# A transformer block on one core: gate and query rows by column groups, first statistics from products of tokens, and another order

## The chip, the core and the metric

The kernel runs on one core of a Trainium2 chip. The metric is device time in microseconds (us), here of that single core. PE is TensorE (matrix products), ACT is ScalarE, DVE is VectorE, POOL is GpSimd, and SP is the queue that issues nearly all DMA transfers. PSUM is the memory that PE writes; this kernel divides its eight banks into four pairs, numbered 0 to 3.

## The reference, cut to what matters

```python
# x: 2048 tokens of 576; 32 heads of 18; the feed-forward is 4608 wide; c is one row of 576
mod = silu(c) @ w_mod                       # six rows: sa, ca, ga, sb, cb, gb
h = layernorm(x) * (1 + ca) + sa
q, k, v = split_heads(h @ wqkv)
phi_q = [softmax(q @ w_phi), softmax(-(q @ w_phi))]      # 36 features a head
phi_k = the same of k
kv, z = phi_k^T v, sum of phi_k over the tokens
x = x + ga * (((phi_q @ kv) / (phi_q . z + 1e-6)) @ wo)
h = layernorm(x) * (1 + cb) + sb
out = x + gb * (relu(h @ w1) @ w2)
```

## The kernel before

The 2048 tokens are 16 tiles of 128. The kernel has two stages.

**The ordered stage** is everything up to the attention of the first two tiles. It is a string ORDER of some 450 short job names, executed from left to right. Each job emits its instructions on its own engine, so ORDER fixes the order on every engine, and semaphores do the rest. `name:n` gives a job PSUM pair n; a job that takes a pair waits until the pair's former contents have been read. The numbers are token tiles or weight chunks:

- `Z` idle products of 512 columns that keep PE going; `sc`, `sh` the columns ca and sa of mod; `FK` folds w_phi into the key weights, `fs fsr` evict them scaled by 1 + ca, `frd fra frr` unscaled (d on DVE, a on ACT); `FQ`, `FQs`, `FQrd`, `FQra` the same for the query weights, by chunk; `wsd` scales the value weights.
- `bn` layernorm statistics of a tile from x_sb on DVE (L238, L239), `sa sp` their roots on ACT and POOL, `T Tc` turn them into four rows that are appended to the fifth chunk of the transposed tokens. The matching rows of the weights come from `KR VR QR` (products), `KRh VRh QRh` (ACT copies), `KRd VRd QRd` (DVE, L467, straight into the weights).
- Per tile: `K` keys (10 products of 288 columns, L271; tiles 0 and 1 as `Ka` and `Kb`), `eK` two exponentials on ACT (L276), `sK` sums of 18 on DVE (L281), `rK` reciprocals on ACT, `pA pM` on POOL, `V` values, `vE` their eviction on DVE (L302), `kv` their product (L321). `kz` ends that sum.
- `Q` queries of a tile, `eQ` their exponentials, `sq` (L333) the write of these to DRAM and `qi` (L336) the read back, each 288 KB on SP's queue. `qs qp qt` finish a tile on DVE, POOL and SP. Six slots of EQ hold the exponentials of Q; slots 4 and 5 are the same bytes as the places that `qi` of tiles 3 and 4 fills.
- `ga gb` the gate rows (10 products each, L357), `gac gbc` their copies (L361) and `wo` wo scaled by ga on POOL (L602); `m2` mod for the second layernorm; `nu nO ot oc W lb lr ap xc ht hd ha` take tiles 0 and 1 through attention, output product and second layernorm to h2, which the feed-forward reads; `wl w2a w2b` load w1 and w2; `tp` differences of w2 on DVE.

**The feed-forward stage** runs over eight blocks b of two tiles: `l1` (L641, L648) and `l2` (L700). Hooks in `l1` of block b finish the queries of the next two tiles (`q_fin`: sum on DVE, product on POOL, transpose by DMA), read later ones back, and compute their attention. At its head stands, before the change, the read back of tiles 3 and 4:

```python
    NB = NT // 2
    for u in range(QF + 1, QF + NL):
        q_in(u)
    for b in range(NB):
```

In l1, the group's DVE step (L657) must have read a PSUM pair before PE's next group enters it.

Of the kernel before, what the change touches and what calls it, by code (L numbers as in the profile page):

```python
# [7 lines left out]
P = 128  # L8
BF16 = mybir.dt.bfloat16
FP32 = mybir.dt.float32  # L10
FP16 = mybir.dt.float16
EPS = 1e-5
ACT = mybir.ActivationFunctionType
ALU = mybir.AluOpType
AXX = mybir.AxisListType.X

S, D, H, DH, DFF = 2048, 576, 32, 18, 4608
NT = S // P
NC = 5
R = 116  # L20
F = NC * R
X0 = 96
NX = X0 + 4
NJ = DFF // P
HD = 288
G6 = ((0, 6), (6, 6), (12, 4), (16, 6), (22, 6), (28, 4))
GR = 108
# [13 lines left out]


ORDER = """
Z11 sx sd rp sc Z2 ca FK Z3 frd2 fs3 fs0 frd1 sh fs2 fsr fs4 frd0 fs1 frr fra4 Ka0:0 shc bn1 fra3 VR:2 wsd4
bn0 KR:1 bn2 sa0 Z6 sp0 KRh wsd2 bn3 KRd sa2 bn4 VRh T0:1 sp2 Z2 Tc0 VRd Kb0 T2:1 Z1 eKa0 wsd3 Ka1:2 wsd0 wsd1
bn5 Kb1 Tc2 V0:0 eKa1 sK0 K3:1 sa4 sK1 rK0 sp4 K2:2 eK3 pA0 pM0 vE0 bn7 T4:0 rK1 V1:1 Tc4 pA1 eK2 sK3 pM1 K4:0
vE1 rK3 kv0 eK4 K5:2 pA3 bn9 pM3 sK2 kv1 eK5 FQ4:1 FQ3:0 FQrd4 FQra3 ga:2 sK4 FQs4 rK2 V2:1 gac bn6 pA2 pM2
FQs3 V4:2 bn8 sa6 rK4 sp6 vE2 V3:0 sa8 pA4 pM4 vE4 T6:1 kv2 vE3 Tc6 FQ0:2 K6:1 wl0 FQs0 FQrd0 sp8 wo3 sK5 kv3
eK6 kv4 wo2 K7:0 bn10 rK5 wo1 T8:2 wl1 gb:1 sK6 Tc8 eK7 pA5 pM5 K8:2 bn13 rK6 gbc K9:0 sK7 wo4 eK8 V5:1 pA6
bn11 pM6 eK9 V6:2 sK8 wo0 rK7 V7:0 vE5 rK8 pA7 sa10 vE6 pA8 pM8 kv5 FQ1:1 vE7 V8:2 FQs1 sK9 FQra1 sp10 V9:0  # L50
pM7 vE8 rK9 T10:1 kv6 bn12 Tc10 FQ2:2 pA9 K10:1 wl2 pM9 FQs2 FQrd2 sa12 vE9 kv7 eK10 K11:2 sp12 bn15 T12:0 kv8
sK10 Tc12 kv9 eK11 K12:1 bn14 V10:0 rK10 eK12 sK11 pA10 pM10 V11:2 vE10 rK11 QR:1 sa14 pA11 sK12 pM11 kv10 wl3
QRh V12:0 vE11 rK12 sp14 QRd pA12 kv11 pM12 vE12 T14:2 Q0:1 Tc14 wl4 K14:2 eQ0 kv12 Q1:0 eK14 qs0 Q2:1 eQ1
sK14 qp0 K15:2 eQ2 qs1 K13:0 eK15 sq2 m2:1 qp1 qi2 eK13 sK15 V13:2 qt0 qt1 w2a0 rK14 sK13 m2c pA14 V14:0 pM14 rK15 rK13
V15:1 vE14 pA13 pM13 vE13 Q3:0 Q4:2 eQ3 pA15 pM15 vE15 kv13 kv14 eQ4 Q5:1 sq3 kv15 eQ5 Q6:0 kz sq4
Q7:2 eQ6 w2a1 sq5 nu1:3 Q8:1 eQ7 nO1 nu0:0 tp0 eQ8 ot1:3 Q9:2 nO0 sq6 w2a2 oc1 sq8 Q10:1 eQ9 sq7 ot0:0 W1:3
w2b2 oc0 tp1 eQ10 W0:2 lb1 sq9 xc1 Q11:0 lr1 lb0 w2b0 xc0 ap1 tp2 Q12:1 lr0 w2b1 eQ11 ap0 ht1:3 sq10 hd1 ha1 ht0:2 sq11
Q13:0 ha0 hd0 Q14:3 eQ13 Q15:2 eQ12 sq13 eQ15 sq12 eQ14 sq15 sq14
"""

@with_exitstack
def tile_block(ctx, tc, a, out):
# [4 lines left out]
    dram = ctx.enter_context(tc.tile_pool(name="dram", bufs=1, space=bass.MemoryType.DRAM))  # L67
    psum = ctx.enter_context(tc.tile_pool(name="ps", bufs=1, space=bass.MemoryType.PSUM))

    def small(shape, dtype, name):  # L70
        return mem.tile(shape, dtype, name=name, tag=name)

    def carve(reg, start, shape):
        n = 1
        for d in shape:
            n *= d
        names = "abcd"[:len(shape)]
        v = reg[:, start:start + n]
        return v.rearrange(f"p ({' '.join(names)}) -> p {' '.join(names)}", **dict(zip(names, shape)))
# [5 lines left out]
    NEQ, NE, NV, NL = 6, 5, 4, 3  # L85
# [4 lines left out]
    E_sb = carve(RT, NV * H * VW, (NE, 2 * D))  # L90
    xT_hi = NE * 2 * D + NV * H * VW
    EQ = carve(RT, xT_hi + 8 * NC * P, (NEQ, 2 * D))
    SLOT = (0, 1, 2, 3, 4, 5, 2, 3, 4, 5, 2, 3, 4, 5, 2, 3)
    EL = carve(RT, RTL, (NL, 2 * D))
    eqd = dram.tile([P, NT, 2 * D], BF16, name="eqd")
    NET = 4
    QF = 2
# [9 lines left out]
    wga = carve(R2[0], 0, (NC, D))  # L107
    wgb = carve(R2[0], 2880, (NC, D))
    wcb = carve(R2[0], 5760, (NC, 640))
    wsb = carve(RE, 0, (NC, 640))  # L110
    wk, wv, wq = (carve(RH, i * 2880, (NC, D)) for i in range(3))

    wo_sb = small([P, NC, D], BF16, "wo_sb")
    ident = small([P, P + 1], BF16, "ident")
    mk = small([P, 1], FP32, "mk")
    mask = small([P, KVW], BF16, "mask")
    epsr = small([1, KVW + P], BF16, "epsr")
    RS = small([P, 6 * GR + NC * NX + NC * P], BF16, "RS")
# [13 lines left out]
    mv = small([P, 2, NT, 2], FP32, "mv")  # L132
# [3 lines left out]
    sc = small([P, 4, NX], BF16, "sc")  # L136
# [24 lines left out]
    act, dve, pool, sp, pe = nc.scalar, nc.vector, nc.gpsimd, nc.sync, nc.tensor  # L161
# [21 lines left out]
    def load_x(t0, n):  # L183
        sp.dma_start(x_sb[:, t0:t0 + n, :], a["xk"][:, t0 * D:(t0 + n) * D].rearrange("p (t d) -> p t d", d=D))
# [7 lines left out]
    def load(eng, dst, name):  # L192
        eng.dma_start(dst, a[name])
# [8 lines left out]
    load(sp, flat(wkT[0:GP]), "wkT")  # L202
    load_xT(0)
    load(sp, flat(wsh), "wsh")
    load_x(0, 2)
    load(sp, flat(wv_raw), "wv")
    load_x(2, 2)
    load_xT(1)
    load_x(4, 2)
    load(sp, epsr[:], "epsr")  # L210
# [9 lines left out]
    load(sp, flat(wgb), "wgb")  # L220
    load_xT(4)
    load(sp, mask[:], "mask")

    pool.memset(zero[:], 0.0)
    pool.memset(eps_t[:], EPS)
    pool.tensor_copy(mk[:], ident[:, P:P + 1])
    pool.memset(m98[:], 0.0)
    pool.memset(sc[:], 0.0)
# [6 lines left out]
    def bn(n, t):  # L235
        s = st[:, t % 4]
        for hf in range(2):
            dve.bn_stats(out=s[:, hf, :], in_=x_sb[:, t, hf * HD:(hf + 1) * HD])  # L238
        dve.bn_aggr(out=mv[:, n, t, :], in_=s)  # L239

    def mods(w, outs, width, bank, idle=None):

# [16 lines left out]
    def v2(ap):  # L259
        return ap.rearrange("p (b f) -> p b f", b=2)  # L260
# [74 lines left out]
    def q_in(u):  # L335
        sp.dma_start(EL[:, u % NL, :], eqd[:, u, :])  # L336
# [14 lines left out]
        q_pool(u)  # L351
        q_turn(u)

    def row_mm(w, pr):
        for k in range(2):
            for ck in range(NC):
                pe.matmul(pr[:, k, 0:HD], lhsT=rep[0:R, ck, :], rhs=w[0:R, ck, k * HD:(k + 1) * HD],  # L357
                          start=(ck == 0), stop=(ck == NC - 1))

    def row_e(pr, dst):  # L360
        act.activation(out=v2(dst[:]), in_=pr[:, :, 0:HD], func=ACT.Copy)  # L361

    def num_mm(t, pr):
        seen = set()
# [53 lines left out]
    G5, FW = 504, 72  # L418
# [9 lines left out]

    last = PS[0:R, 5, 0:NC * FW].rearrange("p (c f) -> p c f", f=FW)

    def f_scaled(dst, ck):
        act.activation(out=dst[0:R, ck, 0:G5], in_=PS[0:R, ck, 0:G5], func=ACT.Copy, scale=ca1[0:R, ck:ck + 1])

# [13 lines left out]
    T1, T2, T4 = (carve(RTh, i * TW, (NK, HD)) for i in range(3))  # L447
# [17 lines left out]
    def rows_d(pr, dst):  # L465

        dve.scalar_tensor_tensor(out=v2(dst[X0:NX, 4, :]), in0=v2(tmpr[X0:NX, :]), scalar=mk[X0:NX, :],  # L467
                                 in1=pr[X0:NX, :, 0:HD], op0=ALU.mult, op1=ALU.add)

    def silu():  # L470
        dve.tensor_scalar(out=sg[0:R, 1, :], in0=sg[0:R, 0, :], scalar1=1.0, scalar2=None, op0=ALU.add)
# [89 lines left out]
    def k_minus(t):  # L561
# [7 lines left out]
    ROWS = {"K": wfold, "V": wv_raw, "Q": wfold}  # L569
    ROWD = {"K": wk, "V": wv, "Q": wq}  # L570
    at = {}
# [6 lines left out]
        "sh": lambda: mods([wsh], None, R, 7, idle=6),  # L578
        "shc": lambda: dve.tensor_copy(m98[0:R, :, X0 + 3], PS[0:R, 7, 0:NC]),
        "FK": lambda: fold_all(wkT),  # L580
        "fs": lambda c: f_scaled(wk, c),
        "frd": lambda c: f_raw(dve, c), "fra": lambda c: f_raw(act, c),
        "fsr": lambda: dve.tensor_tensor(out=wk[0:R, :, G5:D], in0=last,
                                         in1=ca1[0:R, :].unsqueeze(2).to_broadcast([R, NC, FW]), op=ALU.mult),
        "frr": lambda: dve.tensor_copy(out=wfold[0:R, :, G5:D], in_=last),
        "rp": lambda: pool.tensor_copy(rep[0:R], siluc[0:R, :].unsqueeze(2).to_broadcast([R, NC, P])),
        "wsd": lambda c: wv_scale(c, dve), "wsa": lambda c: wv_scale(c, act), "wsp": lambda c: wv_scale(c, pool),
        "bn": lambda t: bn(0, t), "sa": stats_a, "sp": stats_p,
        "T": lambda t: t_cols(t, at["T", t]), "Tc": lambda t: rows_copy(t, at["T", t]),
        "K": lambda t: proj(at["K", t], t, wk), "eK": lambda t: exps(t, at["K", t], E_sb[:, t % NE, :]),  # L590
        "Ka": lambda t: proj(at["Ka", t], t, wk, range(4)), "Kb": lambda t: proj(at["Ka", t], t, wk, [4]),
# [20 lines left out]
        "hd": lambda i: h2_e(i, at["ht", i], dve), "ha": lambda i: h2_e(i, at["ht", i], act),  # L612
        "tp": lambda k: t_part(0, k),
    }
    for w in "KVQ":
        JOBS[w + "R"] = lambda w=w: rows_mm(ROWS[w], at[w + "R", None])
        JOBS[w + "Rh"] = lambda w=w: rows_h(at[w + "R", None])
        JOBS[w + "Rd"] = lambda w=w: rows_d(at[w + "R", None], ROWD[w])
    for w, m, g in (("ga", wga, ga_row), ("gb", wgb, gb_row)):
        JOBS[w] = lambda w=w, m=m: row_mm(m, at[w, None])  # L620
        JOBS[w + "c"] = lambda w=w, g=g: row_e(at[w, None], g)

    ctx.enter_context(tc.manual_schedule())
    for word in ORDER.split():
        name, _, s = word.partition(":")
        f = name.rstrip("0123456789")
        n = int(name[len(f):]) if len(f) < len(name) and name not in JOBS else None
        if name in JOBS:
            f = name
# [104 lines left out]
        sp.dma_start(outf[t * P:(t + 1) * P, :], x_sb[:, t, :])  # L734

    NB = NT // 2
    for u in range(QF + 1, QF + NL):
        q_in(u)
    for b in range(NB):
        t0 = 2 * b + 2  # L740
        more = b + 1 < NB
# [46 lines left out]
def _layout(inputs):  # L788
    import numpy as np
    g = {k: np.ascontiguousarray(np.asarray(v)) for k, v in inputs.items()}  # L790
# [21 lines left out]
    x = g["A_x"].reshape(S, D)  # L812
# [13 lines left out]
    w = g["A_wqkv"]  # L826
# [13 lines left out]
    o["bdw"] = flat(pad(bd.transpose(1, 0, 2), GP))  # L840
    idm = np.zeros((P, P + 1), np.float32)
    idm[:, :P] = np.eye(P)
    idm[X0 + 1, P] = -1.0
    o["ident"] = idm.astype(dt)
    mk = np.zeros((P, KVW), np.float32)
    ep = np.zeros((1, KVW + P), np.float32)
# [38 lines left out]
```

The softmax here doesn't subtract the row's maximum and nothing guards it: scores larger than these inputs give would overflow.

## Time and profile before

| What | Value |
|---|---|
| Median of 8 runs | 403.36 us (401.85 to 404.51) |
| The profiled execution: its own time, and its span | 403.38 us, 401.2 us |
| First product of l1 of block 0 | 101.28 us |
| l1 and l2 of block 0 | 101.28 to 140.62 us (39.34 us) |
| Block 1 | 140.62 to 177.67 us (37.05 us) |
| End of PE's last product | 385.8 us |

The span runs from the first to the last instruction, and 2.2 us of the execution's own time lie around it. The busy time of PE counts overlapping instructions once, and waits inside a pipelined stream do not show in it; so the starts of the products in the timeline say more. A part of the page's chain of waits, and the tables by window, give the same order of events.

### The profile page before, as it was taken

The page shows a single profiled execution, that of the slowest core. Times are in us where ns is not written, and L with a number is a line of the kernel's source. Part 1 is how long each engine was busy: PE and PEld are TensorE (multiplying, and loading weights), DVE is VectorE, ACT ScalarE, POOL GpSimd, SP SyncE. Part 2 cuts the span into 40 slices and gives each one's busy share as a digit, 9 for nine tenths or more (in the row PEclk, how much of TensorE's full clock was granted, in tenths as well). Part 3 has the DMA queues.
Part 4 walks back from the last instruction along what each step waited for, and adds up shares of the span by engine and source line. Part 5 has one row for each costly group of instructions (what it writes and reads, how often), then busy time and mean ns, then how long its engine had stood idle before and what let it go on. Part 6 is the DMA issues. An engine that isn't in the chain of part 4 may idle for free.

```text
span 401.2 us, 8874 instructions
## 1 busy us (share of the span) xinstructions
PE 389.2 (97%) x3679; PEld 314.2 (78%) x3679; DVE 243.5 (61%) x453; ACT 158.1 (39%) x359; POOL 141.5 (35%) x199
## 2 busy tenths in 40 slices
PE   8998999997989999999999999999999999999995
PEld 5677878885868788788878887887888788778874
DVE  1898997556288955664576466646745855654221
ACT  1687886678632135105312331252053214312510
POOL 2147976700110340452055107503630551072044
PEclk9999999999999999999999999999999999999999
DMA  8999134799561124136202613341152013110000
GB/s 272 364 416 417 69 119 178 152 342 406 195 128 24 34 62 105 33 33 105 64 16 63 117 20 34 69 98 34 33 105 34 16 47 61 34 33 31 2 0 32
DMA packets 49131, 44.11 MB, mean 110 GB/s; under 512 B 39281, under 2 KB 41570, under 8 KB 48578
## 3 DMA queue, kind: packets, MB, share of 16 engines
q1 hardware_dynamic: 48818, 43.36, 38.3%
q8 instruction: 29, 0.48, 0.5%
q10 hardware_dynamic: 272, 0.18, 0.1%
q14 instruction: 12, 0.10, 0.1%
HBM read 27.73 MB, written 6.49 MB: 85 GB/s over the span
## 4 chain that ended last, share of the span: by engine, by line
PE 68%; POOL 2%; DVE 0%; issue 0%; POOLq 0%; DVEq 0%
PE PS L641 30%; PE PS L700 28%; PE PS L648 4%; PE PS L398 4%; PE PS L379 1%; POOL RH L712 1%; POOL x_sb L687 1%; POOL yt L686 0%; DVE yt L685 0%; POOLq L881 0%; POOL yt L730 0%; DVE x_sb L733 0%; DVEq L685 0%; POOLq L730 0%; POOLq L712 0%
## 5 line engine op out<-in xcount | busy, mean ns | idle before, releaser
L641 PE MATMUL PS<-h,R 128*128 128x256 bf16 x1152 | 134.0, 273 | 1.8 <-DVE RH L657 1.6
L641 PEld LDWEIGHTS <-R 128*128 128x128 bf16 x1152 | 109.7, 98 | 19.9 <-issue 7.2
L700 PEld LDWEIGHTS <-RH 128*128 128x128 f16 x864 | 84.4, 98 | 21.9
L700 PE MATMUL PS<-R,RH 128*128 128x288 bf16 (+1 forms) x576 | 75.6, 286 | 0.0
L686 POOL TENSOR_TENSOR yt<-yt,gb_row 128x288 f32<-128x288 f32 x23 | 16.8, 730 | 165.7 <-DVE yt L685 165.7
L655 ACT ACTIVATE RH<-PS 128x256 f16<-128x256 f32 x72 | 27.6, 383 | 114.9 <-PE PS L648 108.4
L657 DVE SCALAR_TENSOR_TENSOR RH<-PS,RH 128x256 f16<-128x256 f32 x72 | 30.1, 419 | 68.1 <-ACT RH L655 68.1
L276 ACT ACTIVATE RT<-PS,rs 128x576 bf16<-128x576 f32 x64 | 42.9, 745 | 9.1 <-PE PS L271 5.6
L656 ACT ACTIVATE RH<-PS 128x512 f16<-128x512 f32 x72 | 42.9, 596 | 7.8 <-PE PS L641 6.5
L704 ACT ACTIVATE RS<-PS 128x288 f32<-128x288 f32 x24 | 9.8, 410 | 76.0 <-PE PS L700 76.0
L700 PE MATMUL PS<-RT,RH 128*128 128x288 f16 x288 | 37.9, 286 | 0.0
L271 PE MATMUL PS<-RH,RT 116*128 116x288 bf16 x240 | 31.9, 286 | 0.4 <-DVE h L510 0.2
L271 PE MATMUL PS<-RH,R 116*128 116x288 bf16 x240 | 31.7, 286 | 0.5 <-DVE RH L467 0.3
L712 POOL TENSOR_TENSOR RH<-RH,RT 128x2304 f16<-128x2304 f16 x7 | 31.8, 4542 | 0.0
L271 PEld LDWEIGHTS <-R 116*128 116x128 bf16 x240 | 22.8, 98 | 6.7 <-ACT R L545 0.7
L271 PEld LDWEIGHTS <-RT 116*128 116x128 bf16 x240 | 22.9, 98 | 6.5 <-DVE h L510 0.5
L408 DVE TENSOR_SCALAR xn<-x_sb,mv,rs 128x576 bf16<-128x576 bf16 (+1 forms) x28 | 22.4, 840 | 7.3 <-ACT rs L403 7.3
L238 DVE BATCH_NORM_STATS2 st<-x_sb 128x6 f32<-128x288 bf16 x60 | 24.4, 448 | 1.4 <-DMA x_sb<-in_xk_dram 0.8
L687 POOL TENSOR_TENSOR x_sb<-yt,x_sb 128x288 bf16<-128x288 f32 x31 | 22.7, 732 | 5.9 <-DVE yt L683 4.1
L281 DVE TENSOR_REDUCE Rq<-RT 128x64 f32<-128x1152 bf16 x16 | 21.5, 1342 | 5.2 <-DMA RT<-eqd 3.0
L343 POOL TENSOR_TENSOR ratq<-Rq,rq 128x32 f32<-128x32 f32 x16 | 4.1, 253 | 54.5 <-DVE rq L340 50.6
L398 PE MATMUL PS<-wo_sb,oT 128*128 128x288 bf16 x160 | 22.5, 287 | 0.3 <-ACT oT L607 0.3
(113 smaller groups left out, 437.2 us busy)
## 6 DMA issues: line engine op xcount, KB each, us to landing
R<-in_w1a_dram SPq DMA_DIRECT2D x4, 1152.0 KB, 14.2
eqd<-RT SPq DMA_DIRECT2D x14, 288.0 KB, 5.9
RT<-eqd SPq DMA_DIRECT2D x14, 288.0 KB, 2.9
R<-in_w2a_dram SPq DMA_DIRECT2D x3, 864.0 KB, 7.5
R<-in_w2b_dram SPq DMA_DIRECT2D x3, 864.0 KB, 8.6
out_dram<-x_sb SPq DMA_DIRECT2D x16, 144.0 KB, 1.7
RT<-in_xT_dram SPq DMA_DIRECT2D x2, 640.0 KB, 13.8
x_sb<-in_xk_dram SPq DMA_DIRECT2D x3, 288.0 KB, 8.6
```

The costliest lines, as they stand in the source:

```text
L238: dve.bn_stats(out=s[:, hf, :], in_=x_sb[:, t, hf * HD:(hf + 1) * HD])
L271: pe.matmul(pr[:, k, 0:HD], lhsT=xt(t, ck), rhs=w[0:R, ck, k * HD:(k + 1) * HD], start=(ck == 0), stop=(ck == NC - 1))
L276: act.activation(out=E.rearrange("p (b h s e) -> p b h s e", b=2, s=2, e=DH)[:, :, :, s, :], in_=pr[:, :, 0:HD].rearrange("p b (h e) -> p ...
L398: pe.matmul(pr[:, k, 0:HD], lhsT=oT[:, t % 2, ci, :], rhs=wo_sb[:, ci, k * HD:(k + 1) * HD], start=(ci == 0 and not add_x), stop=(ci == NC ...
L408: dve.tensor_scalar(out=o, in0=i, scalar1=mv[:, 1, t, 0:1], scalar2=rs2[:, t, 0:1], op0=ALU.subtract, op1=ALU.mult)
L641: pe.matmul(PS[:, 2 * u + hf, n * 256:n * 256 + 256], lhsT=w1a[:, ci, jj * P:(jj + 1) * P], rhs=hb[:, ci, :], start=(n == 0 and ci == 0), ...
L655: act.activation(out=A11[:, j, :], in_=lo[:, :, 0, :], func=ACT.Relu)
L656: act.activation(out=A2[:, j, :, :], in_=PS[:, 2 * u + 1, :].rearrange("p (n s f) -> p n s f", n=2, s=2), func=ACT.Relu)
L657: dve.scalar_tensor_tensor(out=U3[:, j, :], in0=lo[:, :, 1, :], scalar=0.0, in1=A11[:, j, :], op0=ALU.max, op1=ALU.subtract)
L687: pool.tensor_tensor(out=x_sb[:, t, c], in0=y, in1=x_sb[:, t, c], op=ALU.add)
L700: pe.matmul(PS[:, bank, 0:HD], lhsT=am[:, j, :], rhs=bm[:, j, :], start=first and j == 0, stop=(j % 9 == 8), skip_group_check=True)
L712: pool.tensor_tensor(out=A12, in0=A12, in1=U2, op=ALU.subtract)
```

## The change

1. **Column groups.** `ga`, `gb` and `QR` had 10 products of 288 columns each, with 128 (100 for `QR`) stationary columns. Now each has 20 products of 144 columns with 32 stationary columns, which go to four groups of 32 PSUM partitions. The eviction then has 144 columns instead of 576. Since the row lies in four pieces on four partition groups, it is put together by DMA: the gate rows are written to DRAM (`gaw`, `gbw`) and read back for all partitions (`gar`, `gbr`); the query rows go by four transfers into the weights (`QRd`; `QRe` is the DVE step).
2. **Statistics of tiles 0 to 3.** `gm` multiplies the transposed tokens of two tiles with themselves (sums of squares are on the diagonal) and with a column of ones: 20 products for two tiles. `bn0` and `bn2` then read them from PSUM with five DVE instructions for two tiles. x_sb of these tiles is loaded after everything else.
3. **Order.** ORDER is another one. Among its differences: 14 idle products instead of 25; `VR` and `m2` stand elsewhere; all `Q` follow `K15`; `qi3` and `qi4` stand in ORDER, and the reads at the head of the feed-forward are gone; the slots of EQ repeat after six tiles instead of four; two of the five scaled key chunks are evicted on DVE; the reads of w2a and the scaling of wo stand elsewhere.

```diff
-Z11 sx sd rp sc Z2 ca FK Z3 frd2 fs3 fs0 frd1 sh fs2 fsr fs4 frd0 fs1 frr fra4 Ka0:0 shc bn1 fra3 VR:2 wsd4
-bn0 KR:1 bn2 sa0 Z6 sp0 KRh wsd2 bn3 KRd sa2 bn4 VRh T0:1 sp2 Z2 Tc0 VRd Kb0 T2:1 Z1 eKa0 wsd3 Ka1:2 wsd0 wsd1
...
-sK10 Tc12 kv9 eK11 K12:1 bn14 V10:0 rK10 eK12 sK11 pA10 pM10 V11:2 vE10 rK11 QR:1 sa14 pA11 sK12 pM11 kv10 wl3
-QRh V12:0 vE11 rK12 sp14 QRd pA12 kv11 pM12 vE12 T14:2 Q0:1 Tc14 wl4 K14:2 eQ0 kv12 Q1:0 eK14 qs0 Q2:1 eQ1
...
-w2b2 oc0 tp1 eQ10 W0:2 lb1 sq9 xc1 Q11:0 lr1 lb0 w2b0 xc0 ap1 tp2 Q12:1 lr0 w2b1 eQ11 ap0 ht1:3 sq10 hd1 ha1 ht0:2 sq11
-Q13:0 ha0 hd0 Q14:3 eQ13 Q15:2 eQ12 sq13 eQ15 sq12 eQ14 sq15 sq14
+Z11 sx sd rp sc FK ca Z2 frd4 fs1 fra1 frd3 sh fs2 frr fs0 fsd3 fra0 fsr fra2 wsd1 wsd2 gm0:0 shc fsd4 gm2:1
+bn0 KR:2 bn2 sa0 sp0 bn4 sa2 Ka0:0 KRh sp2 wsd3 T0:1 Z1 KRd Tc0 T2:1 bn5 Tc2 Kb0 FQ2:2 eKa0 K3:1 FQrd2 wsd0
+FQs2 K2:0 sK0 eK3 VR:2 wsd4 eK2 sK3 m2:1 VRh sK2 rK3 Ka1:0 m2c pA3 rK0 VRd sa4 pM3 Kb1 FQ1:1 bn7 eKa1 V0:2 bn6
+pA0 FQra1 V1:0 sp4 FQs1 vE0 pM0 sa6 sK1 T4:1 V2:2 Tc4 rK2 bn8 pA2 rK1 K4:1 sp6 vE2 pA1 kv0 pM1 vE1 eK4 K5:2
+bn14 T6:0 ga:1 pM2 sK4 Tc6 kv1 eK5 V3:0 bn9 rK4 kv2 gac vE3 pA4 FQ3:2 sa8 K6:1 pM4 FQra3 sK5 FQs3 kv3 eK6 K7:0
+bn11 sp8 bn10 rK5 T8:2 V4:1 Tc8 wl0 pA5 eK7 sK6 pM5 K8:2 sa10 vE4 rK6 K9:0 sK7 sp10 eK8 pA6 wl1 pM6 kv4 bn13
+rK7 V7:1 eK9 sK8 V5:2 pA7 pM7 vE7 rK8 V6:0 vE5 gaw sK9 pA8 V8:1 pM8 vE6 rK9 FQ0:2 gar kv5 FQrd0 gb:0 pA9 kv6
+vE8 w2a2 gbc pM9 kv7 FQs0 FQ4:0 bn15 kv8 T10:1 V9:2 Tc10 FQrd4 wo0 sa14 bn12 FQs4 wl2 K10:1 wo2 vE9 sa12 K11:0
+eK10 sp12 sp14 kv9 eK11 wo3 T12:2 sK10 V10:1 w2a1 Tc12 wo1 sK11 QR:0 rK10 K12:2 QRh pA10 QRe rK11 wl3 vE10
+pM10 K13:0 eK12 V12:1 eK13 sK12 pA11 pM11 kv10 T14:2 sK13 V11:0 wl4 rK12 Tc14 pA12 K14:2 rK13 pM12 vE11 w2a0
+vE12 kv11 eK14 K15:0 pA13 pM13 kv12 sK14 QRd eK15 V13:1 gbw wo4 rK14 V14:2 sK15 pA14 gbr Q0:0 vE13 pM14 rK15
+vE14 kv13 eQ0 Q1:1 pA15 pM15 Q2:2 qs0 eQ1 kv14 eQ2 V15:0 qs1 qp0 Q3:1 sq2 vE15 qp1 qt0 Q4:2 eQ3 qt1 kv15 eQ4
+Q5:0 kz qi2 tp2 Q6:1 eQ5 sq3 tp1 sq4 nu0:2 eQ6 nu1:3 nO0 Q7:0 sq5 sq6 nO1 ot0:1 eQ7 Q8:2 w2b0 tp0 oc0 ot1:3
+Q9:0 eQ8 w2b2 W0:1 eQ9 Q10:2 oc1 lb0 xc0 sq9 Q11:0 lr0 sq8 eQ10 ap0 W1:3 sq7 eQ11 sq10 ht0:1 lb1 w2b1 xc1
+Q12:2 ha0 hd0 lr1 Q13:0 eQ12 ap1 qi3 Q14:1 eQ13 sq12 ht1:3 Q15:2 sq11 ha1 hd1 eQ14 sq13 eQ15 sq14 qi4 sq15
...
-    SLOT = (0, 1, 2, 3, 4, 5, 2, 3, 4, 5, 2, 3, 4, 5, 2, 3)
+    SLOT = (0, 1, 2, 3, 4, 5, 0, 1, 2, 3, 4, 5, 0, 1, 2, 3)
...
+    def gram_mm(t, pr):
+        for j in range(2):
+            for ck in range(NC):
+                x = xt(t + j, ck)
+                pe.matmul(pr[:, j, 0:P], lhsT=x, rhs=x, start=(ck == 0), stop=(ck == NC - 1), skip_group_check=True)
+                pe.matmul(pr[:, j, P:P + 1], lhsT=x, rhs=one[0:R, :], start=False, stop=(ck == NC - 1),
+                          skip_group_check=True)
+    def gram_bn(t, pr):
+        m, v = mv[:, 0, t:t + 2, 0], mv[:, 0, t:t + 2, 1]
+        for j in range(2):
+            dve.scalar_tensor_tensor(out=gd[:], in0=pr[:, j, 0:P], scalar=1.0 / D, in1=ident[:, 0:P], op0=ALU.mult,
+                                     op1=ALU.mult, accum_out=gs[:, j:j + 1])
+        dve.tensor_scalar(out=m, in0=pr[:, :, P], scalar1=1.0 / D, scalar2=None, op0=ALU.mult)
+        dve.tensor_tensor(out=gs[:, 2:4], in0=m, in1=m, op=ALU.mult)
+        dve.tensor_tensor(out=v, in0=gs[:, 0:2], in1=gs[:, 2:4], op=ALU.subtract)
...
-    def row_mm(w, pr):
-        for k in range(2):
-            for ck in range(NC):
-                pe.matmul(pr[:, k, 0:HD], lhsT=rep[0:R, ck, :], rhs=w[0:R, ck, k * HD:(k + 1) * HD],
-                          start=(ck == 0), stop=(ck == NC - 1))
+    QW = D // 4
+    def quarters(pr, lhs, w):
+        for ck in range(NC):
+            for g in range(4):
+                pe.matmul(pr[32 * g:32 * g + 32, 0, 0:QW], lhsT=lhs(ck), rhs=w[0:R, ck, g * QW:(g + 1) * QW],
+                          start=(ck == 0), stop=(ck == NC - 1), skip_group_check=True)
...
+    def quarter_rows(i, dst):
+        for g in range(4):
+            sp.dma_start(dst[X0:NX, 4, g * QW:(g + 1) * QW], part(2 * i + 1)[32 * g + 28:32 * g + 32, :])
...
     NB = NT // 2
-    for u in range(QF + 1, QF + NL):
-        q_in(u)
     for b in range(NB):
```

## The prediction

> **What bounds it now.** I read first the busy table and the slices of the page, then the windows by stage, then PE's waits, then the timeline where PE stops. PE is busy 97% of the span at full clock:
>
> ```profile
> PE 389.2 (97%) x3679; PEld 314.2 (78%) x3679; DVE 243.5 (61%) x453; ACT 158.1 (39%) x359; POOL 141.5 (35%) x199
> PEclk9999999999999999999999999999999999999999
> ```
>
> But idle products and pipelining hide waits in that figure. The windows (length; busy PE, PEld, DVE, ACT, POOL; clock, DMA share, GB/s) show which engine stands beside PE in each stage:
>
> ```profile
> 20.00:40.00 20.00, 18.55 (x185) 14.54 (x184) 17.28 (x31) 16.14 (x40) 12.14 (x30) 1.00 1.02 417
> 40.00:60.00 20.00, 19.87 (x211) 16.22 (x209) 18.78 (x33) 16.50 (x40) 16.86 (x35) 1.00 0.26 97
> 76.60:101.28 24.68, 22.67 (x223) 17.79 (x221) 14.61 (x28) 18.68 (x34) 3.05 (x5) 1.00 0.94 338
> 101.28:140.62 39.34, 37.53 (x350) 30.48 (x348) 27.72 (x49) 13.57 (x30) 6.82 (x9) 1.00 0.39 94
> 140.62:177.67 37.05, 37.05 (x349) 30.36 (x347) 21.72 (x43) 10.61 (x25) 12.84 (x12) 1.00 0.31 59
> ```
>
> Keys and values (20 to 60) load DVE over 90%; the query stretch (76.6 to 101.28) is PE with ACT. Block 0 takes 39.34 us, block 1 37.05 without a wait: 2.3 us are lost in block 0. The timeline says where (start, duration, idle before, releaser):
>
> ```profile
> 105.94 2.27 SPq L336 DMA_DIRECT2D RT<-eqd  x2
> ...
> 110.07 1.35 DVE L281 TENSOR_REDUCE Rq<-RT 128x64 f32<-128x1152 bf16 x1 [3.01 <-DMA RT<-eqd]
> ...
> 111.73 0.36 DVE L657 SCALAR_TENSOR_TENSOR RH<-PS,RH 128x256 f16<-128x256 f32 x1
> ...
> 112.14 0.60 PE L641 MATMUL PS<-h,R 128*128 128x256 bf16 x4 [1.59 <-DVE RH L657]
> ```
>
> Tile 3's read back starts on SP only at 105.94, after all writes; DVE waits for it until 110.07, the relu step queues behind that sum, and PE waits for the relu step.
>
> **Paces.** Ten products of 288 columns take 1.39 us with 0.29 us for the last, so 0.1225 us each and 1.23 us a job, though a row says 286 ns. The Trainium skill, "Perfetto Trace Analysis", Identifying the Most-Contended Engine, says matmul occupancy is a poor measure since matmuls are pipelined; this trace agrees. "TensorE: Matmul & The Clock Gate", Back-to-back issue gap, gives N/2.4 + 2.5 ns, 122.5 ns for 288; it agrees too. From the timeline: ACT pair of exponentials 1.32, DVE sum 1.31, DVE eviction of values 0.75, two bn_stats with aggregate 0.97, kv 0.35.
>
> **The ordered stage before.** From the end of `Kb0` (19.90) to l1 (101.28), 81.4 us, the timeline has these holes in PE's stream: 0.62 round the last idle product; 1.23 at 31.5, where `ga` waits for its weights (1.06 of it put down to DMA); 1.07 round `W1` and `W0`; 1.05 between `ht1` and `ht0`; 0.72 round `Q13` to `Q15`; 0.98 in small ones. Sum 5.67, so 75.7 us of work.
>
> **Change, part by part.**
> *Column groups.* 3 x 10 products at 1.23 us = 3.7 us go; 3 x 20 of 144 columns come. No row of before has one. From below: four groups at once, 5 x 0.0625 = 0.3, say 0.4 us a job; from above: one after another 20 x 0.0625 = 1.25, plus a drain. "TensorEngine Tiling (Array Packing)", Tiling Modes and Restrictions, says column tiles run independently, a mode switch drains, and Fast Weight Load is off; "TensorE: Matmul & The Clock Gate", Part 3, measured 2.38 for three tiles at N=512. At N=144 loads weigh more; the small products with 108 columns follow each other at 0.053 us, load included. I take 0.7, kept 0.4 to 1.6: 3.7 becomes 2.1. The copies shrink from 0.65 us (576 columns) to about 0.3 on ACT, and `QRe` from 0.82 to about 0.35 on DVE.
> *DMA assembly.* Four new gate transfers and four of `QRd`. The gate rows have cover: `gac` ends near 37.5 and `wo0` wants the row near 52; a write and a read at 2 to 3 us each (the 1.2 KB load took 2.1) fit. `gb` is wanted 20 us into the feed-forward. `QRd` is not so safe; see the rivals.
> *Statistics.* Four `bn` (3.9 us DVE) become two `gram_bn` of about 1.3 (two 128-column steps at 0.33, three small at 0.21), and PE gets 2 x 0.9 us (10 x (0.056 + 0.032), the latter m2's pace of one-column products). They lie from 13.15 to 15.0, where before `Ka0` and `VR` ran. x_sb of tiles 0 to 3 frees 576 KB ahead of the loads, 1.4 us at the 417 GB/s shown. So `ga` no longer waits: its weights land near 31.3, it comes near 34.8.
> *Start.* `sh` still waits for its weights (10.9) and ends at 13.15. Then gm 15.0, `KR` to 16.3, `bn2` to 17.45, `T0` 17.7, `KRh` on ACT to 18.75, `Tc0` to 19.1, `KRd` to 19.6, `Kb0` to 19.9. The start gains nothing: `VR` has gone, gm came, and the chain through DVE and ACT ends where it did.
> *Keys and values.* Work after `Kb0`: 75.7 + 1.23 (`VR` is now later) - 0.12 (`T2` earlier) - 1.6 = 75.2. Of it 26.7 belong to `Q0` and after (16 Q 19.6, V15 1.23, kv 1.05, nu 0.76, ot and ht 1.12, W 2.94), 48.5 come before. DVE has in that stretch 16 sums 20.9, 14 evictions 10.4, 11 bn 10.7, others 4.0: 46 us of 48.5, so it must not slip. Following the order with these durations, PE waits 0.25 before `V0` (`VRd`), 0.2 before `T4` (ACT evicting `FQ1`), 0.7 round `K5` and `T6` (`vE2`, `vE1` behind POOL's ratios), about 0.7 elsewhere: 1.8, against 3.0 before. `Q0` starts at 19.9 + 48.5 + 1.8 = 70.2.
> *Moved steps, and what covers them.* `m2` (1.25) moves from 71.7 to about 24; its second weights landed at 25.2 and now 1.4 sooner, so it runs without a wait. `wo` (five of 1.27 on POOL) moves from 39 to 49 to about 52 to 64; POOL has 2.0 us a tile besides, and `pA10` behind them comes near 59.6, half a microsecond before DVE can use it. Two scaled key chunks move to DVE (2 x 0.64), under `sh`. On SP, `w2a2` goes ahead of `wl2`, which must wait for `FQ4` near 52.5 as it waited for `FQ2` at 52.9; `w2a1` and `w2a0` are 20 to 25 us earlier than they were, and take 1.7 MB out of the query stretch, where DMA was 94% busy. x_sb of tiles 0 to 3 lands after all else, near 42, and is first read by `W0` near 86. These cost nothing; without that cover the dearest is `wo`, 6.4 us ahead of `pA10`, and with it `V10`'s pair.
> *Queries.* All 16 now follow `K15`. To the end of `ha1` ACT has 14 eQ 18.5, oc 1.4, xc 1.3, lr 1.0, ha 1.5 = 23.7 us, PE 26.7: PE leads. The slots repeat after six, so the 3.0 us for which exponentials waited for writes to DRAM go. Left are 0.5 at `nu1` (second transpose), 0.8 at `Q14` (`hd0` queues behind `ha0`), 0.6 at l1 (`ha1`, `hd1` after `ht1`): 1.9, against 2.8. So l1 would start 28.6 after `Q0`, at 98.8; I add 0.4 for handoffs not counted: 99.2, gain 2.1.
> *Block 0.* `qi3` and `qi4` are issued before the last writes, near 28 and 32 us after `Q0`; tile 3's sum is due near 35. The wait goes; late next is only ACT's last `eQ15`, 0.5 before its pair is wanted. Of the 2.3 I expect 1.9. Blocks 1 to 7 and the tail are untouched.
> *Sum.* Span 401.2 - 2.1 - 1.9 = 397.2, with the 2.2 around it 399.4 against the execution's 403.38. The median, 403.36, is the same: **399.3**.
>
> **Rivals.**
> *A, the order holds its work better than I count.* With no wait at all from `Kb0` on and 0.4 a group job: 3.7 + 0.4 + 0.9 more, 394.3; half of that is likelier, 396.5. For it: PE ran 40 to 60 with almost no hole. Against: DVE has 2.5 us of room.
> *B, column groups run in turn.* They then do not do what they say: 3 x (1.6 - 0.7) = 2.7 back, 402.0. For it: no trace shows them at once.
> *C, DVE becomes the bound.* If its 46 us stretch by 6% with handoffs, `Q0` moves by 2.5 to 3: 402.0. For it: 18.78 of 20 busy; against: 6 us of DVE's work moved to before 20 or left.
> *D, slower: the query rows come late.* `QRd` stands on SP behind `wl3`, `wl4` and `w2a0`, which can only be issued once `QR` has read wfold, near 59.5; it goes at 61 to 62, behind 2.6 MB. `Q0` needs it for its fifth chunk, at 71.2. At the 370 KB/us of the same loads before, it lands at 68.5. But the landing times spread:
>
> ```profile
> R<-in_w1a_dram SPq DMA_DIRECT2D x4, 1152.0 KB, 14.2
> R<-in_w1b_dram SPq DMA_DIRECT2D x1, 576.0 KB, 7.8
> ```
>
> With 14.2 us it lands at 76, PE idles 4.8 with every query behind it: 404.1. It decides from 75.3 on, where it eats the whole 4.0. "DMA: Bandwidth & Descriptors", Latency and other measured facts, puts the fixed cost at about 2 us; the trace's 2.1 agrees, so only the queue can do it. Against: 14.2 was measured with DMA full for 15 us.
>
> **How the numbers follow.** Forecast 0.62 (397.4 to 401.2), A 0.13, B 0.10, C 0.07, D 0.08. A measurement can tell about 0.3%, 1.2 us. Faster: forecast and A whole, half of B and C: 0.83. Same: the rest of B and C and a little of D: 0.09. Slower: D and a late C: 0.08. The range 396.0 to 403.3 covers the forecast, half of A, B and C.
>
> **What would show it.** Right: l1 starts at 98.5 to 100; block 0 near 37.4 with no wait on the sum of tile 3; group jobs at 0.7; no wait of `ga` on DMA; `Q0` near 70. Wrong: group jobs over 1.2 (B); DVE without gaps from 25 to 66 and PE waiting for `vE` (C); PE idle inside `Q0` on a DMA into the query weights (D); l1 after 101.

## The result, and the profile after

| What | Before | After |
|---|---|---|
| Median, runs of one chip | 403.20 us (401.42 to 406.69, 32 runs) | 395.11 us (394.65 to 397.42, 11 runs) |
| Ratio, 95% interval | | 0.9805 [0.9788, 0.9822] |
| The profiled execution: own time, span | 403.38, 401.2 us | 394.87, 393.1 us |
| End of `Kb0` | 19.90 | 19.15 |
| First product of `Q0` | another order | 67.98 |
| First product of l1 of block 0 | 101.28 | 95.34 |
| From there to the end | 299.93 | 297.75 |

The kernel takes 1.95% less time (interval 1.8 to 2.1%), twice the gain that was forecast (4.0 us), and lies below the low end of the range. From profile to profile the gain is 8.1 us: 0.75 up to `Kb0`, 5.2 from there to l1, 2.2 in block 0 and behind. `Kb0` is said to end where the product behind it starts.

In part of the executions of most experiments with the new order PE had half its clock for some 3 to 14 us, mostly near the start, which adds up to 6 us, so I compare the stretches of the traces behind it more than medians.

The busy table and the clock of the changed kernel say little again: PE's share rises from 97 to 98% while its busy time falls by 3.9 us, under half of the gain. The rest are holes that closed.

```profile
PE 385.3 (98%) x3738; PEld 312.7 (80%) x3738; DVE 243.2 (62%) x456; ACT 156.6 (40%) x358; POOL 140.9 (36%) x200
PEclk9999999999999999999999999999999999999999
```

The windows by stage (length; busy PE, PEld, DVE, ACT, POOL; clock, DMA share, GB/s):

```profile
20.00:40.00 20.00, 19.78 (x248) 15.96 (x247) 18.98 (x35) 17.79 (x47) 11.21 (x30) 1.00 1.02 414
40.00:60.00 20.00, 20.00 (x243) 16.30 (x241) 17.08 (x27) 15.39 (x41) 18.47 (x40) 1.00 0.62 210
67.98:95.34 27.36, 27.05 (x264) 21.77 (x262) 17.13 (x32) 23.73 (x43) 5.93 (x10) 1.00 0.73 234
95.34:132.55 37.21, 37.21 (x348) 30.47 (x348) 30.27 (x52) 12.81 (x29) 6.44 (x9) 1.00 0.39 104
132.55:169.60 37.05, 37.05 (x349) 30.35 (x347) 22.49 (x44) 10.61 (x25) 12.88 (x12) 1.00 0.27 59
```

From 20 to 40 PE is busy 19.78 instead of 18.55. From 40 to 60 DVE has slack, and DMA, little used there before, carries twice the data; the query stretch has 0.3 us of holes in 27.36. Block 0 (37.21) is now within 0.2 us of block 1 (37.05), which is as it was to the hundredth.

The column groups, on the timeline of PE (start, duration, line, operation, count):

```profile
33.70 0.28 PE L592 MATMUL PS<-ident,sc 128*100 128x128 bf16 x2
33.90 0.50 PE L384 MATMUL PS<-R,RS 116*32 116x144 bf16 x20
34.33 0.52 PE L345 MATMUL PS<-RT 128*128 128x76 bf16 x9
```

`ga` starts at 33.90 and the next job at 34.33: 20 products in 0.43 us. Its first and its last product start 0.27 us apart, a mean of 14 ns, where one of 144 columns alone needs 62 at the pace of the prediction. The single starts in the trace show why: the four products of a chunk, one for each group, start within 10 ns of each other, and the four of the next chunk follow 61 to 63 ns behind them (73 to 75 the first time). So the four groups run at once, each at the pace of 62. There is no wait for weights ahead of it. In the list of PE's waits from 19 to 96 us two are left, one of them ahead of `Kb0`, inside the start:

```profile
PE PS L295 <- DVE RH L503: 0.4, 1, 0.4
PE PS L698 <- DVE h L560: 0.2, 1, 0.2
```

And the place where block 0 lost its time, the read back of tile 3, on SP, PE and DVE:

```profile
93.46 0.32 SPq L360 DMA_DIRECT2D RT<-eqd  x1
...
99.05 0.32 SPq L360 DMA_DIRECT2D RT<-eqd  x1
...
99.28 5.41 PE L698 MATMUL PS<-h,R 128*128 128x256 bf16 x48
...
100.68 1.34 DVE L305 TENSOR_REDUCE Rq<-RT 128x64 f32<-128x1152 bf16 x1
...
102.33 0.36 DVE L714 SCALAR_TENSOR_TENSOR RH<-PS,RH 128x256 f16<-128x256 f32 x1
```

The read goes out 1.9 us ahead of l1, not 4.7 behind its start as before. The sum has nothing in brackets, so it waited for nothing; the relu step behind it is done 7.4 us after l1's start (before: 10.8), and PE's 48 products run through.

### The profile page after: what moved, and what is told of

The parts are those of the page before. It is cut to its first block, busy times and chain, and to the rows that moved or that the text cites. A ratio compares the mean times of both kernels' runs of the same rounds, so it can differ in the third digit from the quotient of the medians.

```text
span 393.1 us, 9008 instructions
## 1 busy us (share of the span) xinstructions
PE 385.3 (98%) x3738; PEld 312.7 (80%) x3738; DVE 243.2 (62%) x456; ACT 156.6 (40%) x358; POOL 140.9 (36%) x200
## 4 chain that ended last, share of the span: by engine, by line
PE 92%; ACT 3%; DVE 2%; DMA 2%; issue 1%; SPq 0%; DVEq 0%; ACTq 0%
PE PS L698 33%; PE PS L757 32%; PE PS L295 12%; PE PS L431 5%; PE PS L705 5%; DMA R<-in_wkT_dram 2%; PE PS L412 2%; PE PS L345 1%; ACT RT L300 1%; PE PS L459 0%; PE PS L239 0%; ACT h L558 0%; ACT yt L499 0%; PE PS L384 0%; PE PS L273 0%
## 5 line engine op out<-in xcount | busy, mean ns | idle before, releaser
L305 DVE TENSOR_REDUCE Rk<-RT 128x64 f32<-128x1152 bf16 x16 | 21.2, 1339 | 4.3 <-ACT RT L300 4.3
L244 DVE BATCH_NORM_STATS2 st<-x_sb 128x6 f32<-128x288 bf16 x52 | 21.1, 448 | 0.5
```

What stands on the lines that cost most here:

```text
L305: dve.tensor_reduce(out=Rr, in_=E.rearrange("p (c e) -> p c e", e=DH), axis=AXX, op=ALU.add)
```

## The experiments

The stretches of all runs, from their traces (us). `FK` is the first product of the folded weights, which starts when a load has landed and varies by itself; the two runs of the changed kernel differ by 0.5 there and agree behind it.

| Kernel | FK to end of `Kb0` | `Kb0` to `Q0` | `Q0` to l1 | l1 to end | Median, ratio to before |
|---|---|---|---|---|---|
| before | 11.27 | 81.38 to l1 | | 299.93 | |
| after | 10.81 | 48.83 | 27.36 | 297.75 | 395.11, 0.9805 |
| after again (e11) | 10.80 | 48.83 | 27.40 | 297.89 | 395.51, 0.9795 [0.9768, 0.9822] |
| e1 groups in turn | half clock | 49.51 | 27.36 | 297.84 | 396.94, 0.9856 [0.9820, 0.9893] |
| e2 wide rows | 10.79 | 51.62 | 27.36 | 297.98 | 398.54, 0.9900 [0.9868, 0.9931] |
| e3 reads at the head | half clock | 48.83 | 27.37 | 297.44 | 395.36, 0.9782 [0.9761, 0.9804] |
| e4 that, and old slots | 10.80 | 48.84 | 32.30, with 3.4 at half clock | 297.99 | 400.21, 0.9915 [0.9882, 0.9947] |
| e5 before, new slots | 11.31 | 80.24 to l1 | | 298.16 | 401.12, 0.9925 [0.9902, 0.9948] |
| e6 statistics from x | 12.56 | 49.69 | 27.49 | 297.64 | 399.95, 0.9896 [0.9867, 0.9926] |
| e7 order and slots alone | half clock | 52.62 | 27.36 | 298.05 | 401.80, 0.9955 [0.9932, 0.9977] |
| e8 `VR` in the hole | 10.81 | 48.84 | 27.35 | 297.78 | 398.39, 0.9846 [0.9798, 0.9894] |
| e9 idle products back | 10.81 | 49.49 | 27.82 | 297.70 | 396.32, 0.9814 [0.9785, 0.9843] |

### Column groups: e1 (in turn) and e2 (wide rows as before)

```diff
 e1, in quarters()
-        for ck in range(NC):
-            for g in range(4):
+        for g in range(4):
+            for ck in range(NC):
```

> The changed kernel with one edit: the twenty products of ga, gb and QR go group by group (five chunks into one group of 32 partitions, then the next), not round the groups. Theory: the jobs took 0.43 us because four column groups ran at once, and PE is the path through the whole ordered stage; in turn a job takes 20 x 0.0625 = 1.25 us, so three jobs add 2.4 us: about 397.5. Rival 1 (the jobs are short because their products are small, not because they run at once): 0.43 stays, 395.1. Rival 2 (other engines' waits take up what PE saves): the jobs get longer, but the time rises by less than 1: 395.1 to 396.

```diff
 e2
+        for k in range(2):
+            for ck in range(NC):
+                pe.matmul(pr[:, k, 0:HD], lhsT=rep[0:R, ck, :], rhs=w[0:R, ck, k * HD:(k + 1) * HD], ...)
...
-        act.activation(out=gt[:, k, :], in_=pr[:, 0, 0:QW], func=ACT.Copy)
+        act.activation(out=v2((ga_row, gb_row)[k][:]), in_=pr[:, :, 0:HD], func=ACT.Copy)
```

`gaw gar gbw gbr` go, and `QRd` takes the place of `QRe`.

> The changed kernel with the gate and query rows as before (10 products of 288 columns each, eviction of 576 columns, no DMA assembly), all else as changed. Theory: PE gets 3 x (1.23 - 0.43) = 2.4 us more and has no room, so about 397.5; the wider evictions on ACT and DVE (0.35 and 0.5 us) are hidden or add a few tenths. Rival (the new order would have waited there anyway): under 1 us, 395.1 to 396.

The same place on PE's timeline, of e1:

```profile
38.33 0.72 PE L384 MATMUL PS<-R,RS 116*32 116x144 bf16 x20
38.99 0.52 PE L345 MATMUL PS<-RT 128*128 128x76 bf16 x9
```

and of e2:

```profile
33.99 1.39 PE L390 MATMUL PS<-R,RS 116*128 116x288 bf16 x10
35.22 0.51 PE L345 MATMUL PS<-RT 128*128 128x76 bf16 x9
```

A job takes 0.43 us with the groups in alternation, 0.66 when they are issued one after another, 1.23 wide. Neither the 1.25 of the theory nor the 0.43 of rival 1 came. In e1 the groups still don't run in turn: its 20 starts, 26 ns apart in the mean, sort into four chains of five, one for each group it seems (the records don't name the group), each with 62 to 63 ns from product to product (73 at first), and the chains begin 79 ns apart; 3 x 79 ns and the 0.26 us of the last chain make the 0.50 from first to last start. So a group keeps its own pace, and the others run beside it in either order of issue. The stretch from `Kb0` to `Q0` grows by 0.68 in e1, which is 3 x 0.23: in this trace each saving arrives in full. It was taken in an execution with half clock in the start; the four at full clock (396.6 to 397.1) lie 1.5 us above those of e3 (395.3), run on the same chip, so 0.8 us of e1 are not located. In e2 it grows by 2.79, of which 3 x 0.80 = 2.40 are the products; the rest are small waits, the plainest 0.4 at `K13`, which waits for the PSUM pair that DVE's wider query row reads. So column groups are worth 2.8 us on the path. What they would cost if one group waited for the other no run shows.

### The reads and the slots: e3, e4, e5

I held that block 0 gained because `qi3` and `qi4` are issued earlier. e3 puts the reads back to the head of the feed-forward; e4 also puts the old slots back; e5 gives only the slots of six to the kernel before.

```diff
 e3 and e4 (ORDER without qi3 and qi4)
+    for u in range(QF + 1, QF + NL):
+        q_in(u)
 e4 as well; e5, on the kernel before, the other way round
-    SLOT = (0, 1, 2, 3, 4, 5, 0, 1, 2, 3, 4, 5, 0, 1, 2, 3)
+    SLOT = (0, 1, 2, 3, 4, 5, 2, 3, 4, 5, 2, 3, 4, 5, 2, 3)
```

> The changed kernel with the reads back of tiles 3 and 4 again at the head of the feed-forward, slots of six kept. Theory: tile 3's sum on DVE waits for the read again and PE waits for the relu step behind it, 1.5 to 2.1 us in block 0: 396.6 to 397.2. Rival (block 0 was mended by the slots, since ACT no longer waits for writes): about 395.4.

> As the kernel with the reads at the head, and the slots of EQ again repeat after four tiles. Theory: the exponentials wait for writes to DRAM again (3.0 us on ACT before), of which PE feels about 1 since ACT stands close beside PE in the query stretch: 397.6 to 398.4. Rival (the slots cost nothing): equal to the kernel with the reads at the head. Rival (all of ACT's wait lands on PE): 399.6 to 400.2.

> The kernel before with one edit: the slots of EQ repeat after six tiles; its order and its reads at the head of the feed-forward stay. Theory S (slots): the exponentials no longer wait for writes to DRAM, so the last of them end some 2 us after the start of l1 instead of 4.2; the last writes and the read of tile 3 follow, and the wait in block 0 goes (2.0 us), with up to 1 us more between Q0 and l1: 400.2 to 401.4. Theory O (it takes the new order as well): 402.5 to 403.4, and the wait in block 0 stays.

The theory fell with e3. Its timeline round the sum of tile 3:

```profile
104.70 0.88 SPq L360 DMA_DIRECT2D RT<-eqd  x2
...
107.75 3.77 PE L698 MATMUL PS<-h,R 128*128 128x256 bf16 x33
108.63 1.35 DVE L305 TENSOR_REDUCE Rq<-RT 128x64 f32<-128x1152 bf16 x1 [1.04 <-DMA RT<-eqd]
...
110.29 0.36 DVE L714 SCALAR_TENSOR_TENSOR RH<-PS,RH 128x256 f16<-128x256 f32 x1
```

The sum does wait 1.04 us for the read, yet PE runs on: the relu step ends at 110.65, 8.5 us after l1's start at 102.16, while PE, which stood still from 9.3 us after l1's start in the kernel before (112.14 - 1.59 - 101.28), had to wait there until 10.8. Block 0 loses nothing, 297.44 to the end. So with slots of six the place of the reads is free; the last writes must be early. Why they were late before is in ACT's waits, here of the kernel before from 70 to 106 us (engine, line, releaser: total, times, longest):

```profile
ACT RT L276 <- DMA eqd<-RT: 3.0, 2, 1.8
```

An exponential waits until the write of the former tile of its slot has left. With the old slots all tiles from 2 on share four slots, and the last exponentials ended 4.2 us after l1's start; 1.2 of the 3.0 us lie there, ahead of these last ones, and 1.8 in the query stretch. The changed kernel has no such line at all; e4, with the old slots back, has, from 68 to 101 us:

```profile
ACT RT L300 <- DMA eqd<-RT: 5.2, 2, 3.0
```

and PE stands behind ACT for a PSUM pair, in e4's list of PE's waits:

```profile
PE PS L295 <- ACT RT L300: 3.4, 2, 2.1
```

There the 4.9 us fall into the query stretch, 32.30 instead of 27.36. The two waits of PE are 3.4 of them; the rest is its clock, which was at half from 95.20 to 98.61, behind the second wait (3.4 us at half, worth 1.7). The two executions of e4 without it (398.93 and 399.07, mean clock 1.000 and 0.999) lie 3.7 above the usual 395.3 of e3. That is more than the theory's 1; the median of 400.21 comes to the range of the last rival only with the half clock. Block 0 is clean (297.99), though slots and reads are the old ones: in the new order PE stands behind these exponentials before l1, and the last of them end 2.1 us after its start, as in the changed kernel. In e5 the line of ACT is gone as well, and of the old order's time 1.14 us go from `Kb0` to l1 and 1.77 behind l1's start: 2.9 in the trace, 0.0075 of 404 = 3.0 in the medians. Its sum of tile 3 still waits for the read, and PE is served in time:

```profile
108.18 1.35 DVE L281 TENSOR_REDUCE Rq<-RT 128x64 f32<-128x1152 bf16 x1 [1.45 <-DMA RT<-eqd]
...
109.83 0.36 DVE L657 SCALAR_TENSOR_TENSOR RH<-PS,RH 128x256 f16<-128x256 f32 x1
```

So one line of the change, the list of slots, is worth 2.9 us in the old order and 3.4 to 3.7 in the new (4.9 with the half clock that followed the wait). In the old order it is what mends block 0; in the new one the wait would only have moved ahead of l1.

### The statistics: e6, and order with slots alone: e7

```diff
 e6
-... fra2 wsd1 wsd2 gm0:0 shc fsd4 gm2:1
-bn0 KR:2 bn2 sa0 ...
+... fra2 wsd1 wsd2 shc fsd4
+bn0 bn1 KR:2 bn2 bn3 sa0 ...
```

x_sb of tiles 0 to 3 is loaded early again. e7 is e2 and e6 together, so that of the change only the order and the slots are left.

> The changed kernel with the statistics of tiles 0 to 3 from x_sb again (four bn on DVE in place of gm and two gram steps), the tokens loaded where they were before; order else unchanged. Theory: the start is a chain through DVE; four bn of 0.97 us take 1.3 us more there than the two gram steps (2.6), and the weights behind the tokens land 1.4 us later, so Kb0 ends 1.3 to 2 later: 396.4 to 397.1. Rival (PE is what the start waits for, and 1.6 us of gm go): 394 to 395. The stretch from Q0 on is unchanged in either case.

> New order, new slots and reads in the order, but gate and query rows and the statistics of tiles 0 to 3 as before. If the parts add up, it is the changed kernel plus what the wide rows cost (2.8 us between Kb0 and Q0 in the trace) plus what bn_stats from the tokens cost in the start (theory: 1.3 to 2): 399.2 to 400, so the order and the slots alone are worth 3 to 4 us of the 8. Rival (the two new computations are what lets the order work): over 401.

The timeline of DVE and ACT in the start of e6, from the first statistics of tile 0 to the copy of the key rows:

```profile
14.69 0.81 DVE L244 BATCH_NORM_STATS2 st<-x_sb 128x6 f32<-128x288 bf16 x2
...
18.31 0.21 DVE L245 BATCH_NORM_AGGREGATE mv<-st 128x2 f32<-128x12 f32 x1
...
19.21 0.64 ACT L499 ACTIVATE yt<-PS 4x576 bf16<-4x576 f32 x1
```

and of the changed kernel:

```profile
14.12 0.28 DVE L259 SCALAR_TENSOR_TENSOR gd<-PS,ident 128x128 bf16<-128x128 f32 x1
...
16.41 0.16 DVE L263 TENSOR_TENSOR mv<-gs 128x2 f32<-128x2 f32 x1
...
17.27 0.64 ACT L499 ACTIVATE yt<-PS 4x576 bf16<-4x576 f32 x1
```

Statistics of four tiles take DVE 3.83 us (14.69 to 18.52) from x_sb, 2.45 (14.12 to 16.57) from products; roots, key rows and `Kb0` follow. Counted from FK, `Kb0` ends 1.75 us later in e6. The tokens, loaded earlier there, are not the reason: up to `Q0` PE's list of waits in e6 has none on a DMA. The 0.86 us more up to `Q0` is another thing: PE waited 2.35 us for the rows of tile 2, and ran at half clock behind that wait (windows of e6; the 0.50 is the clock):

```profile
21.00:22.00 1.00, 1.00 (x9) 0.92 (x8) 0.85 (x3) 0.48 (x1) 0.00 (x0) 0.50 1.01 416
...
24.00:26.00 2.00, 2.00 (x18) 1.75 (x17) 0.85 (x3) 1.60 (x3) 0.00 (x0) 0.99 1.05 429
```

e7 agrees: its stretch from `Kb0` to `Q0` is 3.79 us longer than the changed kernel's, and 2.79 (e2) + 0.86 (e6; the half clock lasts until 24.0 there and until 24.6 in e7) leaves 0.14. So the two computations don't disturb each other. Against e5, which has the old order with the same slots, e7 is no faster: 0.9955 [0.9932, 0.9977] against 0.9925 [0.9902, 0.9948]. Its median, 401.80, lies in the range of the rival, its trace in that of the theory. No execution of e7 had a mean clock above 0.995, so the order's own worth is not settled by this. The two quickest, 400.46 at 0.994 and 0.995, lie 0.7 below e5's median, and a full clock would give them 0.6% of 399, or 2.4 us, at most: between nothing and some 3 us. The three parts measured in traces make 2.79 + 2.91 + 1.75 = 7.45 of the 8.1, and FK's earlier start 0.29, which leaves 0.4; with the slots at their worth in the new order nothing is left. The parts lean on each other, so this sum doesn't settle it either.

### A hole filled: e8

The start still has a wait of 1.06 us behind `T0`. e8 puts `VR` there in place of the idle product.

```diff
-... KRh sp2 wsd3 T0:1 Z1 KRd Tc0 T2:1 ...     K2:0 sK0 eK3 VR:2 wsd4 ...
+... KRh sp2 wsd3 T0:1 VR:3 KRd Tc0 T2:1 ...   K2:0 sK0 eK3 wsd4 ...
```

> The changed kernel with the products VR moved into PE's hole of 1.4 us after T0, in pair 3, which is free until kv0; the idle product there goes. Theory: PE is the path from Kb0 on, so its 1.23 us leave the path and nothing comes back: 393.9 to 394.2. Rival (m2 then waits for its weights, or K2 for the exponentials, as they come 1.2 us earlier): 394.6 to 395.1.

`VR` fits in, `Kb0` comes no later, and yet `Kb0` to `Q0` is 48.84. PE's waits of e8 from 20 to 69 us tell where the 1.2 us went:

```profile
PE PS L273 <- DMA RE<-in_wsb_dram: 0.9, 1, 0.9
PE PS L295 <- ACT RT L300: 0.5, 1, 0.5
```

`m2`, moved up by the length of `VR`, is now ahead of its weights, and a key job ahead of the exponentials that free its PSUM pair. Work moved into a hole in front of two other limits gains nothing.

### Idle products: e9, and the changed kernel again: e11

```diff
-Z11 sx sd rp sc FK ca Z2 frd4 ...
+Z11 sx sd rp sc Z2 FK ca Z3 frd4 ...
```

> The changed kernel with five idle products put back in its head: two stand again behind `sc`, three behind `ca`, 16+3 instead of 11+2+1 ahead of `gm`. Theory (idle products at the start are what keeps the clock that the throttle grants at full while PE waits for the first weights): every execution has a mean granted clock of 0.993 or more, none is some 4 to 6 us longer than the rest, and in the usual execution `Kb0` ends within 0.3 us of the changed kernel's 19.15, since PE waits there for DMA and the idle products lie in that wait: median 394.8 to 395.6. Rival 1 (idle products at the head cost time of PE, which is why there are fewer): `Kb0` ends 5 x 0.21 = 1.1 us later, 396.2. Rival 2 (the lower clock comes from late weights alone, whatever PE does meanwhile): executions with a mean clock of 0.981 to 0.987 as in the other kernels with this order, 399 to 401 in these.

> The changed kernel as it is, for comparison on the same chip with the five idle products put back. Its usual execution takes 395.1 us. Theory (fewer idle products leave the start open to a lower clock): of its executions one or more has a mean clock below 0.99 and is 4 to 6 us longer, where the kernel with the five put back has none. Rival (this start is as safe as any, and the low clocks seen came with the edits of the other runs): no execution below 0.993, all within 1.5 us of 395.1.

This was inconclusive. Neither kernel showed a low clock in these executions (0.997 or more in all nine), so the frequency of it can't be compared. The idle products cost nothing at the start (10.81 from FK, as without). The 0.8 us between the medians isn't shown to be theirs: in the profiled execution of e9 `m2` waited 1.0 us for its weights, and l1 waited 0.7 for `hd1` instead of 0.2. Why the weights came later there stays open.

## Why the prediction was wrong, by its own steps

The mechanisms were mostly right and nearly every size was too small, on one side. Against the forecast gain of 4.0 us in the profiled execution stand 8.1:

| Term | Forecast | Measured | Gain missed |
|---|---|---|---|
| End of `Kb0` | 19.9 | 19.15 | 0.75 |
| A group job (three) | 0.7 | 0.43 | 0.8 |
| PE's waits from `Kb0` to `Q0` | 1.8 | 1.1 | 0.7 |
| PE's waits from `Q0` to l1 | 1.9 | 0.65 | 1.25 |
| Handoffs not counted | 0.4 | none | 0.4 |
| Block 0 and behind | gain 1.9 | gain 2.2 | 0.3 |

The waits measured are the stretch less the work of the prediction: 48.83 less 48.5 - 3 x 0.27 = 47.7, and 27.36 less 26.7.

- **The steps that failed are the waits counted after the change, 1.8 + 1.9 + 0.4.** They make 2.35 of the 4.1 missed. Counted were 3.7 us of waits and 0.4 of handoffs, measured 1.75 in all. I followed the new order on paper with each engine's durations end to end. Rows of the timeline start 0.1 to 0.2 us ahead of the end of the row before on the same engine, so such a sum adds up lateness that isn't there; that this is the whole of the difference is likely, not shown. Of the named waits `nu1`'s is none instead of 0.5, `Q14`'s about 0.3 instead of 0.8, and l1's about 0.4 instead of 0.6, of which the list of waits shows 0.22.
- **The group job** was taken inside its bounds, but too near the middle. The lower bound, 0.4, was four groups at once, which is what the change sets up and what the Trainium skill ("TensorEngine Tiling (Array Packing)", Tiling Modes and Restrictions) says of independent tiles; 0.43 and the starts in fours agree with it. The drain at a change of mode, which the same page names, is not seen as such: from the last start to the next job's first lie 0.16 us. Rival B took the order of issue for the order of running: issued group by group, the job took 0.66 in e1, not 1.25 and more, as the groups ran beside each other all the same.
- **The start** was said to gain nothing. "Then gm 15.0" was the step: `gm2` ended at 14.45, and `bn0` reads the first pair while PE still multiplies the second, so `bn2` was done at 16.57, not 17.45, and `KRh` at 17.91, not 18.75. Without the products of tokens `Kb0` comes 1.75 us later (e6); I had set them against the old order, where they only replaced `VR` and `Ka0`. And 0.29 of the 0.75 is luck: FK, which waits for a load, began that much earlier in this execution, and in the other run of the changed kernel it began 0.2 later than before.
- **Block 0**: the size was nearly right by luck, since the cause was not. "`qi3` and `qi4` are issued before the last writes" does nothing (e3). The wait goes because the last exponentials, and with them the last writes and reads, come earlier against l1: the slots of six alone do that (e5), and so does the new order alone, at 3.4 to 4.9 us in the query stretch (e4). I had credited the slots only with the 3.0 us of ACT's waits, and all of it to the query stretch; 1.2 of it lay behind l1's start, and block 0's wait was the tail of the same thing.
- **Cover that held**: `ga` no longer waits for weights, as forecast. `m2` runs without a wait in the changed kernel, but its cover is thin (1.0 in e9, 0.9 in e8). DVE (rival C) had 17.08 of 20 from 40 to 60. `QRd` (rival D) was issued at 58.5 and not at 61 to 62, and the four w1a loads landed in 8.6 us at the median instead of 14.2; PE shows no wait at `Q0`. Rival A, "with no wait at all and 0.4 a group job", 394.3, was the nearest, and had 0.13; the half of it that was called likelier is 396.8 by its own sum of 5.0, not 396.5.

## What to carry to other kernels

When a change removes waits, don't refill the new order with waits worked out by adding whole durations; the rows overlap, and a long ordered stream whose engines each have slack can run with almost none. Look up how many places a ring of buffers has before looking at where its transfers are issued: one list of slots was worth 2.9 us in the old order and 3.4 or more in the new, the place of the reads, with that list, nothing. And a saving inside a stream that PE leads arrives in full (e1: 3 x 0.23 gave 0.68), while work moved into a hole only does so if the next limit is behind it (e8).

## What the runs showed of the hardware that was not expected

- Four products of 144 columns with 32 stationary columns, each for another column group, start within 10 ns, and each group then takes its next product 61 to 63 ns later (73 to 75 the first time), the pace of 144 columns alone (starts of `ga`, `gb` and `QR` in the trace of the changed kernel). Issued group by group (e1), the groups still overlap, with 79 ns from one group's first start to the next group's: 0.66 us for 20 products instead of 0.43.
- PE's clock fell to half behind waits of PE that were not long, and stayed there for whole multiples of 3.41 us (once, once, three, three and four times), as the clock in windows of these traces shows:

| Run | Waits of PE over 0.3 us shortly ahead | Half clock from, to | Length |
|---|---|---|---|
| e1 | 0.86, 0.94 | 11.23, 21.47 | 10.24 |
| e3 | 1.49, 1.18 | 11.00, 24.65 | 13.65 |
| e4 | 1.31, 2.07 | 95.20, 98.61 | 3.41 |
| e6 | 1.73, 2.35 | 20.61, 24.02 | 3.41 |
| e7 | 0.40, 1.74 | 14.34, 24.58 | 10.24 |

In the slices of e7 it is the second and third digit (10 to 30 us):

```profile
PEclk9779999999999999999999999999999999999999
```

The Trainium skill, "TensorE: Matmul & The Clock Gate", Part 1: The HAM clock gate, says the clock halves after an idle window of about 3.4 us and comes back after as much sustained work. The half agrees, and 3.41 as the unit of the lengths. Two things do not: no wait here was longer than 2.35 us, and in e1 and e3 PE was busy by its rows through three and four such lengths and stayed at half. The length of one wait doesn't decide it either: the changed kernel had one of 1.06 us in its start and e6 one of 1.73, both at full clock. What does stays open. 14 idle products instead of 25 in the start are a candidate that e9 could not test, and e4's case, far from the start, can't come from them.
